# First batch by pairs of heads on a queue of its own, dummy products early, 4-byte products spread wider

## The chip, the cores and the metric

The kernel runs on one core of a Trainium2 chip. The time is device microseconds of one execution, from the launch's first to its last instruction with what lies around them; lower is better. Before the change the median of three runs is 395.43 us (393.86 to 397.88).

## The reference: linear attention, then a gated mixer of tokens and channels

Eight batches, eight heads, 576 tokens, head width 64, so a model width of 512 and a hidden width of 2048. All inputs and the output are float32.

```python
# attention, for each batch and head
kv  = k.T @ v                                  # 64 x 64, no softmax
o   = q @ kv                                   # 576 x 64
x   = o / sqrt(mean(o * o, axis=-1) + 1e-6) * g_norm
# heads side by side: x is 576 x 512 for each batch
tok = w_tok @ (alpha1 * x + beta1)             # over the 576 tokens
u   = x + lam * tok
ch  = relu((alpha2 * u + beta2) @ w_ch1) @ w_ch2   # 512 -> 2048 -> 512
out = u + lam * ch
```

## The kernel before

**Layout.** Of a batch's 576 tokens, 512 stand as four rows on each of 128 partitions (token 4p + c is row c of partition p). The last 64 are the tail; tails of two batches share a tile. q, k and v are used as 4-byte fp32r operands of TensorE, everything after the norm as bf16.

**A recorded program.** Every operation is put on record with what it reads and writes, its cost in a table and its priority. `schedule` (line 109) then plays the five engines against that table and writes out one fixed order for each; `synchronize` adds the semaphore waits, and `emit` the instructions. On the chip each engine goes through its order and waits where it must: an instruction that waits holds up all behind it on its engine. A number in the table changes only the order.

**Two streams on TensorE.** "main" is the channel mixer: `ch1` (line 900, 64 products of 512 columns for a batch), `ch1_tail` (line 913, in odd batches) and `ch2` (line 928, 64, and 16 more for the tails). "fill" is the rest, taken up where its inputs are there: `kv` (lines 616 and 621, 20 products a batch), `qtr` (lines 668 and 650, q transposed through a product with the identity, 20), `norm` (lines 701 and 727, q times kv, 20), `tok` (line 800, 20 of 512 columns) and `tok_tail` (line 818). The attention and token mixing of batch b+2 are filled into the channel mixer of batch b. An operation of many 4-byte products (`slow=True`) is woven with one of the main stream, product by product (`woven`, line 293): four with four alternate, the ten of half a `kv` come two or three at a time.

**After a product.** ScalarE squares (line 755), VectorE sums, inverts, scales into `xm` (line 766) and multiplies with e1 into bf16 `rm` or `rtl` (line 770). GpSimd multiplies `xm` with g_norm (line 778). `bias1` (line 786) and the result of `tok` (line 807) are added on VectorE. From batch 2 on, GpSimd makes a2 in two steps (lines 878 and 881) and a transposing DMA puts it where `ch1` reads it; in batches 0 and 1 TensorE transposes (line 838). After `ch2` VectorE scales (line 944), GpSimd adds (line 949), SP stores.

**The head of the program** is batch 0, with no main stream to fill. SP's queue loads q whole, then k and v in two halves of four heads each, as float32; VectorE and ScalarE round k and v to fp32r (lines 599 and 602). GpSimd's queue loads, and converts, the weights: two quarters of w_ch1 at once, and w_tok when the second half of k has landed. Six rows are broadcast over the partitions by products with a row of ones (line 555): e1, g, e2, lam, a2 and b2. `columns` (line 564) turns two rows into columns. Five `wt_group`s transpose w_tok (lines 974 and 976); its row sums are products with a column of ones (lines 1004 and 1008) and wait for all of w_tok. Then come `tok` of batch 0 in two halves of 256 columns (line 800), the transposes of line 838, and the main stream. Batch 1's k and v come as float32 through SP, into the same buffers as batch 0's, and are rounded by VectorE and ScalarE too; later batches come through GpSimd's queue, already as fp32r.

Of the kernel before, what the change touches and what calls it, by code (L numbers as in the profile page):

```python
# [16 lines left out]
DH = 64  # L17
# [35 lines left out]
class Prog:  # L53
    ENGINES = ("PE", "ACT", "DVE", "POOL")

    def __init__(self, nc, stack):
        self.nc, self.stack = nc, stack
        self.ops, self.lastw, self.readers = [], {}, {}
        self.ps = stack.enter_context(nc.psum_tensor("ps", [128, 8, 512], F32))
        self.eng = {"PE": nc.tensor, "ACT": nc.scalar, "DVE": nc.vector,  # L60
                    "POOL": nc.gpsimd, "SP": nc.sync}
        self.pools = {"main": (0, 1, 2, 3), "fill": (4, 5, 6, 7), "any": tuple(range(8))}
        self.main, self.fill = [], []
        self.bias = 0.0
        self.dma_rate = 360e3

# [3 lines left out]
    def _add(self, o, r, w, after):  # L70
        self.ops.append(o)
        for key in r:
# [48 lines left out]
    def schedule(self):  # L121
# [15 lines left out]
        last_fill = False  # L137
# [52 lines left out]
        while left:  # L190
            moved = True
            while moved:
                moved = False
                for e, q in queues.items():
                    if free[e] > t + 1e-9:
                        continue
                    for o in q[:160]:
# [8 lines left out]
                if free["PE"] <= t + 1e-9:  # L206
                    m = main[0] if main and can(main[0], t) else None
                    f = None
                    if not (last_fill and m):
                        for o in fill[:10]:  # L210
# [6 lines left out]
                    if f is not None and m is not None and f.kind == "w":  # L217
# [5 lines left out]
                        take(m, t, cost)  # L223
                        free["PE"] = t + cost
                        self.sequence.append((f, m))
                    elif f is not None:
                        fill.remove(f)
                        take(f, t)
                        free["PE"] = t + f.cost
                        self.sequence.append((f,))  # L230
                        last_fill = True
                    elif m is not None:
# [3 lines left out]
                        self.sequence.append((m,))  # L236
                    else:
                        continue
                    events.add(free["PE"])
# [12 lines left out]
    def synchronize(self):  # L252
# [25 lines left out]
        for unit in self.sequence:  # L278
            for o in unit:
                wait_for(o)  # L280
            for o in self.ended(unit):
# [11 lines left out]
    def woven(f, m):  # L293

        out, i, j = [], 0, 0
        n, k = len(f.fns), len(m.fns)
        while i < n or j < k:
# [3 lines left out]
            else:  # L301
                out.append((m, j))
# [3 lines left out]
    def ended(self, unit):  # L306
        if len(unit) == 1:
            return unit
        f, m = unit
        return (m, f) if self.woven(f, m)[-1][0] is f else (f, m)  # L310

    def emit(self):
# [8 lines left out]
        for unit in self.sequence:  # L321
            for o in self.ended(unit):
# [21 lines left out]
        def _(gps):  # L344
            for unit in self.sequence:
                if len(unit) == 1:
                    o, = unit
                    waits(o)
                    for fn in o.fns:
                        ins = fn(self.eng[o.q])  # L350
                    signal(o, ins)
                    continue
                begun = set()
                for o, i in self.woven(*unit):
                    if o.idx not in begun:
                        begun.add(o.idx)
                        waits(o)
                    ins = o.fns[i](nc.tensor)
# [7 lines left out]
def bass_transnormer_attn__then__resmlp_affine_kernel(  # L366
# [15 lines left out]
    with ExitStack() as stack:  # L382
# [7 lines left out]
        identb = sb("identb", [128, 128], BF16)  # L390
        ones = sb("ones", [128, 128], F32)
# [75 lines left out]


        P.bias = -1000.0
        P.op("DVE", dve(2), lambda e: e.memset(eps[:], 64e-6), w=["eps"])  # L470
# [10 lines left out]
        for i in range(2):  # L481
            P.op("POOL", pool(1024, 0), lambda e, i=i: e.memset(kvc[:, i].bitcast(F32), 0.0),
                 w=[("kvc", i, j) for j in range(2)])
# [7 lines left out]
        P.dma("SP", "q", 1 << 20, lambda e: e.dma_start(md(q0), src_main(q, 0, 0, 8)),  # L491
              w=["q0"])
        P.dma("SP", "qtl", 1 << 17, lambda e: e.dma_start(q0t, src_tail(q, 0, 0, 8)),
              w=["q0t"])
        first = {}
        for h in range(2):
            a, z = 4 * h, 4 * h + 4
            for n, x, m, tl in (("k", k, kst, kstt), ("v", v, vst, vstt)):
                first[n, h] = P.dma("SP", "%sm%d" % (n, h), 1 << 19,
                                    lambda e, x=x, m=m, a=a, z=z: e.dma_start(  # L500
                                        md(m[:, a:z]), src_main(x, 0, a, z)),
                                    w=[("st", n, h)])
                P.dma("SP", "%st%d" % (n, h), 1 << 16, lambda e, x=x, tl=tl, a=a, z=z:
                      e.dma_start(tl[:, a:z], src_tail(x, 0, a, z)), w=[("stt", n, h)])
        for i, x in enumerate((moe_alpha1, moe_lam, moe_beta1, moe_alpha2, moe_beta2)):
            P.dma("ACT", "row%d" % i, 2048, lambda e, i=i, x=x: e.dma_start(
                rows[0:1, i, :], x[None, :]), w=[("row", i)])
        P.dma("ACT", "row5", 256, lambda e: e.dma_start(rows[0:1, 5, 0:DH], g_norm[None, :]),
              w=[("row", 5)])
# [4 lines left out]
            w=["wl"], after=[first["k", 1]], issue=1.2)  # L514
# [15 lines left out]

        load_w1(0)
        load_w1(1)
# [20 lines left out]
        def broadcast(i, dst, key, n=DM):  # L553
            t = P.bank("fill")
# [6 lines left out]
        def columns():  # L561

            t = P.bank("fill")
# [8 lines left out]
        def fill_q(b):  # L572

            if b > 1:
                load_kv(b)
# [6 lines left out]
        def load_kv(b):  # L582
            for n, x, m, tl in (("k", k, kr, krt), ("v", v, vr, vrt)):
                P.dma("POOL", n + "r", 1 << 20, lambda e, x=x, m=m: e.dma_start(
                    md(m[:]), src_main(x, b, 0, 8)), w=[(n, 0), (n, 1)], issue=1.2)
# [3 lines left out]
        def round_kv(h, both=False):  # L589
            a, z = (0, 8) if both else (4 * h, 4 * h + 4)  # L590
            hs = (0, 1) if both else (h,)
# [546 lines left out]
```

## Time and profile before

| what | value |
|---|---|
| median of three runs | 395.43 us |
| the profiled execution | 393.75 us, of which the span is 391.9 us |
| TensorE busy | 365.0 us, 93% of the span |
| VectorE, ScalarE, GpSimd busy | 195.2, 163.0, 198.6 us |
| first product of the channel mixer | 57.92 us after the span's start |
| last product | ends at 387.28 us |
| read from HBM, written | 38.04 MB, 9.44 MB |

A busy TensorE is not one at its peak: a product counts from its start to its modelled end, so neighbours overlap, and a product at half clock is as busy as one at full clock. The spacing from one start to the next says more. The granted clock is printed as full from the start; where the spacing says otherwise, the text goes by the spacing.

### The profile page before, as it was taken

How to read it: one execution, taken by the hardware profiler on the slowest of the kernel's cores; microseconds unless marked ns; L12 is line 12 of the kernel's file. 1: busy time of each engine (PE TensorE's matmuls, PEld its weight loads, DVE VectorE, ACT ScalarE, POOL GpSimd, SP SyncE). 2: the span in 40 equal slices, each digit the busy share in tenths (PEclk: the TensorE clock that was granted, in tenths of full speed). 3: DMA queues.
4: the chain of work that ended last, by engine and by line, in shares of the span. 5: the costliest groups of instructions: out<-in, count | busy, mean ns of one | idle time of the engine just before them, and what ended most of it. 6: DMA issues, size and time to landing. Idle time of an engine off the chain costs nothing.

```text
span 391.9 us, 5426 instructions
## 1 busy us (share of the span) xinstructions
PE 365.0 (93%) x2163; PEld 219.4 (56%) x2163; DVE 195.2 (50%) x329; ACT 163.0 (42%) x323; POOL 198.6 (51%) x180
## 2 busy tenths in 40 slices
PE   3568799999999998998999998899999999999995
PEld 3344678545768566466565774756444644444642
DVE  3244871894259479758849647255970020010042
ACT  3243617901695145472186252446017305406500
POOL 7112604332526996898897697564878131031000
PEclk9999999999999999999999999899999999999999
DMA  8999587900492965659649149801103021020012
GB/s 229 229 232 316 84 134 142 221 2 9 139 302 36 269 138 131 125 107 253 147 83 240 26 102 259 178 16 40 55 29 79 15 80 56 0 79 30 2 54 80
DMA packets 62118, 46.52 MB, mean 119 GB/s; under 512 B 28615, under 2 KB 57351, under 8 KB 62092
## 3 DMA queue, kind: packets, MB, share of 16 engines
q0 software_dynamic: 34240, 27.27, 40.3%
q1 hardware_dynamic: 27840, 18.88, 18.8%
q8 instruction: 17, 0.28, 0.3%
q14 instruction: 9, 0.07, 0.1%
q10 hardware_dynamic: 12, 0.01, 0.0%
HBM read 38.04 MB, written 9.44 MB: 121 GB/s over the span
## 4 chain that ended last, share of the span: by engine, by line
PE 72%; DVE 11%; DMA 8%; POOL 3%; issue 2%; ACT 2%; SPq 2%
PE ps L928 25%; PE ps L900 24%; PE ps L800 8%; DMA xm<-in_v_dram 4%; DMA vrt<-in_v_dram 4%; PE ps L913 3%; PE ps L616 3%; DVE rm L770 3%; PE ps L701 2%; PE ps L668 2%; POOL a1f L878 2%; PE ps L555 1%; DVE xm L766 1%; DVE small L758 1%; DVE rtl L770 1%
## 5 line engine op out<-in xcount | busy, mean ns | idle before, releaser
L900 PE MATMUL ps<-a2m,w 128*128 128x512 bf16 x512 | 132.3, 386 | 0.0
L928 PE MATMUL ps<-w,ht 128*128 128x512 bf16 x512 | 127.5, 382 | 0.0
L895 ACT ACTIVATE ht<-ps 128x512 bf16<-128x512 f32 x128 | 76.2, 598 | 84.3 <-PE ps L900 83.0
L928 PEld LDWEIGHTS ps<-w,ht 128*128 128x128 bf16 x512 | 49.3, 98 | 51.7 <-issue 0.4
L900 PEld LDWEIGHTS ps<-a2m,w 128*128 128x128 bf16 x512 | 49.2, 98 | 48.8 <-issue 0.8
L944 DVE TENSOR_TENSOR tmp<-ps,lam_bc 128x512 f32<-128x512 f32 x36 | 24.8, 688 | 97.9 <-PE ps L928 97.8
L949 POOL TENSOR_TENSOR xm<-xm,tmp 128x512 f32<-128x512 f32 x28 | 37.1, 1326 | 57.5 <-DVE tmp L944 57.4
L778 POOL TENSOR_TENSOR xm<-xm,g_bc 128x512 f32<-128x512 f32 x32 | 43.6, 1374 | 31.9 <-DVE rm L770 31.8
L758 DVE TENSOR_REDUCE small<-sq 128x8 f32<-128x512 f32 (+2 forms) x41 | 26.8, 661 | 39.8 <-ACT sq L755 39.7
L878 POOL TENSOR_TENSOR a1f<-xm,a_bc 128x512 f32<-128x512 f32 x24 | 30.1, 1271 | 17.2 <-DVE xm L807 17.2
L701 PE MATMUL ps<-kvc,qt 128*128 128x128 f32 x128 | 37.6, 412 | 1.2 <-ACT lam_bc L558 1.2
L616 PE MATMUL ps<-vr,kr 128*128 128x128 f32 x128 | 27.5, 349 | 10.5 <-ACT vrt L602 3.8
L800 PE MATMUL ps<-rm,wt 128*128 128x512 bf16 (+1 forms) x144 | 35.2, 372 | 0.7 <-DVE rtl L770 0.5
L881 POOL TENSOR_TENSOR a2b<-a1f,b_bc 128x512 bf16<-128x512 f32 x27 | 34.1, 1271 | 0.3
L786 DVE SCALAR_TENSOR_TENSOR xm<-e_bc,wsum,xm 128x512 f32<-128x512 f32 (+1 forms) x36 | 32.4, 942 | 1.6 <-POOL xm L778 1.4
L668 PE MATMUL ps<-identr,qr 128*128 128x128 f32 x112 | 32.0, 395 | 1.3 <-DVE kvc L632 1.3
L616 PEld LDWEIGHTS ps<-vr,kr 128*128 128x128 f32 x128 | 24.2, 220 | 13.6 <-DMA vrt<-in_v_dram 4.4
L755 ACT ACTIVATE sq<-ps 128x512 f32<-128x512 f32 (+2 forms) x41 | 23.5, 582 | 14.5 <-PE ps L701 9.4
L673 ACT ACTIVATE qt<-ps 128x512 fp32r<-128x512 f32 x32 | 19.2, 600 | 24.6 <-PE ps L668 19.0
L701 PEld LDWEIGHTS ps<-kvc,qt 128*128 128x128 f32 x128 | 26.2, 217 | 4.5 <-ACT kvc L635 1.5
L770 DVE TENSOR_TENSOR rm<-xm,e_bc 128x512 bf16<-128x512 f32 x32 | 27.2, 862 | 0.1
L807 DVE TENSOR_TENSOR xm<-ps,xm 128x512 f32<-128x512 f32 (+1 forms) x36 | 21.5, 624 | 10.8 <-PE ps L800 10.6
(107 smaller groups left out, 396.3 us busy)
## 6 DMA issues: line engine op xcount, KB each, us to landing
out_dram<-xm SPq DMA_DIRECT2D x32, 256.0 KB, 2.4
qr<-in_q_dram POOLq DMA_DIRECT2D x7, 1024.0 KB, 11.0
kr<-in_k_dram POOLq DMA_DIRECT2D x6, 1024.0 KB, 6.8
vr<-in_v_dram POOLq DMA_DIRECT2D x6, 1024.0 KB, 9.5
w<-in_moe_w_ch_dram POOLq DMA_DIRECT2D x8, 512.0 KB, 10.2
ht<-in_q_dram SPq DMA_DIRECT2D x1, 1024.0 KB, 5.6
xm<-in_k_dram SPq DMA_DIRECT2D x2, 512.0 KB, 9.9
xm<-in_v_dram SPq DMA_DIRECT2D x2, 512.0 KB, 12.7
```

The lines of the kernel that those rows point to most:

```text
L616: fns += [lambda e, h=h, o=o, c=c: e.matmul(t.ap()[:, o], fl(kr[:, h, c:c + 2, :]), fl(vr[:, h, c:c + 2, :]), start=(h % 4 == 0 and c == 0 ...
L668: fns.append(lambda e, h=h, c=c, o=o: e.matmul(t.ap()[:, o], fl(qr[:, h, c:c + 2, :]), identr[:], start=True, stop=True))
L701: fns = [lambda e, h=h: e.matmul(t.ap()[:, 128 * (h % 4):128 * (h % 4) + 128], qt[:, h, cp, :], kvc[:, i, h, :], start=True, stop=True) fo ...
L770: P.op("DVE", dve(n), lambda e: e.tensor_tensor(out=r, in0=x, in1=bc(e1_bc[rs, fs]), op=ALU.mult), r=xks + ["e1"], w=rks)
L778: P.op("POOL", pool(n), lambda e: e.tensor_tensor(out=hv(gx), in0=hv(gx), in1=gv, op=ALU.mult), r=xks + ["g"], w=xks)
L800: lambda e, sc=sc: e.matmul(t.ap()[:, cs], wt[:, sc if sc < 4 else tail_w(b), 128 * c:128 * c + 128], (rm[:, b % 2, sc, cs] if sc < 4 else ...
L878: P.op("POOL", pool(512), lambda e: e.tensor_tensor(out=a1f[:, s], in0=x, in1=a2_bc[:], op=ALU.mult), r=ks + ["a2"], w=[("a1f", s)])
L881: P.op("POOL", pool(512), lambda e: e.tensor_tensor(out=a2b[:, c], in0=a1f[:, s], in1=b2_bc[:], op=ALU.add), r=[("a1f", s), "b2"], w=[("a2 ...
L895: P.op("ACT", act(512), lambda e: e.activation(dst, t.ap(), ACT.Relu), r=[t], w=keys, pri=-1000)
L900: P.mm("main", 512, [lambda e, dj=dj: e.matmul(t.ap(), w1[:, dj, 128 * fj:128 * fj + 128], a2m[:, b % 3, dj, :], start=(dj == 0), stop=(dj ...
L928: P.mm("main", 512, [lambda e, fj=fj, t=t, c=c: e.matmul(t.ap(), (ht[:, fj, 128 * c:128 * c + 128] if c < 4 else hl[:, fj, :]), w2[:, fj, ...
L949: lambda e: e.tensor_tensor(out=x, in0=x, in1=tmp[:, s], op=ALU.add),
```

## The change

**First batch by pairs of heads.** k, v and q of batch 0 come as four DMAs each, of two heads, in the order k, v, q for each pair, behind the two tails, all on SP's queue. w_tok now waits for the third pair of k, and the w_ch1 quarters are recorded later, behind it. `round_kv`, `kv`, `qtr` and `norm` work on a pair of heads in batch 0. `kv` is recorded as a group of four products for each pair and a group of one or two for the tails, in all batches. `norm` takes one pair with all four rows, where it took four heads with two rows.

**Fewer steps in the head.** lam, a2 and b2 are loaded by broadcasting DMAs once the third quarter of w_ch1 has landed. The row sums of w_tok are taken group by group, each with its own wait. Batch 1's k and v come through GpSimd's queue as in later batches, without rounding. In batch 0 GpSimd makes two of the four `rm`. The second half of the tail's transposed w_tok is written by ScalarE.

**Dummy products.** A zeroed 128x256 bf16 tile is multiplied with itself on TensorE, with nobody reading the result, wherever the schedule sees TensorE idle before the first true product: 47 products.

**The weave.** A group of more than two 4-byte products for batch b+2 is spread over two operations of the main stream, eight products, where a second one is ready. The cost table is changed: a woven 4-byte product counts 74 ns, or 58 ns where spread over two, and early products count double. DMAs of GpSimd's queue keep the order in which they are recorded. Work of batch 0 may use seven PSUM banks instead of four.

```diff
-                        cost = sum(max(len(o.fns) * 0.056, o.cost * (0.53 if o is f else 1))
-                                   for o in (f, m))
+                        cost = m.cost + 0.074 * n
...
+                        if (n > 2 and f.pri // 100 - (m.pri - 150) // 100 > 1 and m2 is not None and not m2.narrow
+                                and can(m2, t + cost)):
+                            main.pop(0)
+                            unit.append(m2)
+                            take(m2, t + cost, m2.cost - 0.016 * n)
+                            cost += m2.cost - 0.016 * n
...
+                    elif self.warm is not None and t >= self.warm[0].end and not begun:
+                        o = Op("PE", "m", 0.11, 0.0, [self.warm[1]], 0.0, len(self.ops))
...
+        P.warm = (P.op("DVE", dve(256), lambda e: e.memset(warm[:], 0.0), w=["warm"]),
+                  lambda e: e.matmul(P.ps[:, 3, 0:256], warm[:, 0:128], warm[:],
+                                     start=True, stop=True))
...
+        def pair_dma(eng, n, x, m, hp):
+            first[n, hp] = P.dma(eng, "%s%d" % (n, hp), 1 << 18, lambda e: e.dma_start(
+                md(m[:, 2 * hp:2 * hp + 2]), src_main(x, 0, 2 * hp, 2 * hp + 2)),
+                w=[("st", n, hp)])
...
+        for hp in range(4):
+            pair_dma("SP", "k", k, kst, hp)
+            pair_dma("SP", "v", v, vst, hp)
+            pair_dma("SP", "q", q, q0, hp)
...
-            w=["wl"], after=[first["k", 1]], issue=1.2)
+            w=["wl"], after=[first["k", 2]], issue=1.2)
...
-        load_w1(0)
-        load_w1(1)
...
+            for hp in hps:
+                fns = []
+                for h in (2 * hp, 2 * hp + 1):
...
+                P.mm("fill", 128, fns, r=[("k", hp), ("v", hp)], w=[t], slow=True)
...
+            swap = b == 0 and hp in (0, 2)
+            P.op("POOL" if swap else "DVE", pool(n) if swap else dve(n),
+                 lambda e: e.tensor_tensor(out=r, in0=x, in1=bc(e1_bc[rs, fs]), op=ALU.mult),
+                 r=xks + ["e1"], w=rks, pri=-300 if swap else 0)
...
-        P.op("DVE", dve(8), lambda e: e.memset(wsum[:], 0.0),
-             r=[("wtm", i) for i in range(6)] + ["wt45"], w=["wt", "wsum0"])
...
-        broadcast(1, lam_bc, "lam")
-        broadcast(3, a2_bc, "a2")
-        broadcast(4, b2_bc, "b2")
...
+        load_w1(0)
+        load_w1(1)
+        fill_q(1)
         load_w1(2)
         load_w1(3)
-        fill_q(1)
         for i in range(4):
             load_w2(i)
+        for x, dst, key in ((moe_lam, lam_bc, "lam"), (moe_alpha2, a2_bc, "a2"),
+                            (moe_beta2, b2_bc, "b2")):
+            P.dma("SP", "b" + key, 1 << 18, lambda e, x=x, dst=dst: e.dma_start(
+                dst[:], x.partition_broadcast(128)), w=[key], after=[wdma[2]])
...
+        P.cold = 22.0
```

In the rows of an order below, `ht` and `xm` hold the float32 q, k and v of batch 0, `kr`, `vr` and `qr` the fp32r ones, `w` any of the weights or rows; `128x2x256` is two heads on 128 partitions.

SP's queue at the start of the program, before:

```order
L491 DMA ht<-in_q_dram 128x8x256
L493 DMA ht<-in_q_dram 64x8x64
L500 DMA xm<-in_k_dram 128x4x256
L504 DMA xt<-in_k_dram 64x4x64
L500 DMA xm<-in_v_dram 128x4x256
L504 DMA tmp<-in_v_dram 64x4x64
L500 DMA xm<-in_k_dram 128x4x256
```

and after:

```order
L541 DMA xt<-in_k_dram 64x8x64
L545 DMA tmp<-in_v_dram 64x8x64
L537 DMA xm<-in_k_dram 128x2x256
L537 DMA xm<-in_v_dram 128x2x256
L537 DMA ht<-in_q_dram 128x2x256
L537 DMA xm<-in_k_dram 128x2x256
L537 DMA xm<-in_v_dram 128x2x256
```

Whole q no longer stands ahead of k and v; the last pair of q is the last of the fifteen loads. On GpSimd's queue the first DMA is now w_tok's, behind its wait for the third pair of k; the w_ch1 quarters, which stood ahead of it without a wait, follow it.

TensorE from its first true product on; before (identity and `ht` are q's transposes, `vr,kr` is `kv`, `w,ones` a broadcast, `kvc,qt` is `norm`):

```order
L665 MATMUL ps<-ident,ht 128x128 x16
L645 MATMUL ps<-ident,ht 128x64 x4
L616 MATMUL ps<-vr,kr 128x128 x8
L621 MATMUL ps<-vrt,krt 128x2x64 x2
L555 MATMUL ps<-w,ones 128x512
L555 MATMUL ps<-w,ones 128x64
L555 MATMUL ps<-w,ones 128x512
L701 MATMUL ps<-kvc,qt 128x128 x8
L727 MATMUL ps<-kvc,qtt 128x128 x2
L616 MATMUL ps<-vr,kr 128x128 x8
L621 MATMUL ps<-vrt,krt 128x2x64 x2
L555 MATMUL ps<-w,ones 128x512 x3
```

and after, around the last pair of q (`ht` in the third row) and the first of five groups of w_tok's transpose (`identb`):

```order
L657 MATMUL ps<-vr,kr 128x128 x4
L665 MATMUL ps<-vrt,krt 128x2x64
L711 MATMUL ps<-ident,ht 128x128 x4
L657 MATMUL ps<-vr,kr 128x128 x4
L747 MATMUL ps<-kvc,qt 128x128 x4
L665 MATMUL ps<-vrt,krt 128x2x64
L1023 MATMUL ps<-identb,ht 128x128 x4
L1025 MATMUL ps<-identb,hl 128x64
```

and behind the fifth group (`ones,w` is `columns`, `onesb,wt` the row sums):

```order
L747 MATMUL ps<-kvc,qt 128x128 x4
L772 MATMUL ps<-kvc,qtt 128x128 x2
L596 MATMUL ps<-w,ones 128x512
L605 MATMUL ps<-ones,w 128x1 x8
L1054 MATMUL ps<-onesb,wt 128x1 x4
L1057 MATMUL ps<-onesb,wt 64x1 x2
```

Behind the last pair of q stand now one `kv`, two `norm`s, w_tok's transposes, one broadcast of 512 columns, `columns` and the row sums; then `tok` of batch 0.

TensorE in the channel mixer, `kv` of a later batch, before:

```order
L616 MATMUL ps<-vr,kr 128x128 x2
L900 MATMUL ps<-a2m,w 128x512
L616 MATMUL ps<-vr,kr 128x128 x3
L900 MATMUL ps<-a2m,w 128x512
L616 MATMUL ps<-vr,kr 128x128 x2
```

and after, batch 3's `kv` in batch 1's `ch2` (line 977 now):

```order
L665 MATMUL ps<-vrt,krt 128x2x64
L977 MATMUL ps<-w,ht 128x512 x2
L665 MATMUL ps<-vrt,krt 128x2x64
L977 MATMUL ps<-w,ht 128x512 x2
L657 MATMUL ps<-vr,kr 128x128
L977 MATMUL ps<-w,ht 128x512 x2
```

and the end of batch 3's attention, ahead of batch 2's `ch1` (line 949 now):

```order
L714 MATMUL ps<-identr,qr 128x128
L977 MATMUL ps<-w,hl 128x512
L714 MATMUL ps<-identr,qr 128x128 x4
L696 MATMUL ps<-identr,qrt 128x64 x4
L747 MATMUL ps<-kvc,qt 128x128 x16
L949 MATMUL ps<-a2m,w 128x512 x4
```

A 4-byte product has two of the main stream between it and the next, where it had one or stood in a cluster. At the end of batch 3's attention 24 stand alone: batch 1's `ch2` has no product left there, and batch 2's `ch1` stands behind them. Over the whole program the fill of the last batch ends some 210 main products later than before.

More of the change, by code (lines that the diff above doesn't have):

```diff
@@ L196, in schedule @@
                         continue
-                    for o in q[:160]:
+                    held = False
+                    for o in list(q):
+                        if o.kind == "d":
+                            if held:
+                                continue
+                            held = e == "POOL"
                         if can(o, t):
@@ L278, in synchronize @@
         for unit in self.sequence:
-            for o in unit:
-                wait_for(o)
-            for o in self.ended(unit):
+            for o, first, last in self.steps(unit):
+                if first:
+                    wait_for(o)
+                if not last:
+                    continue
                 count[o.q] += 1
@@ L292, in woven @@
     @staticmethod
-    def woven(f, m):
+    def woven(unit):
+        if len(unit) == 1:
+            return [(unit[0], i) for i in range(len(unit[0].fns))]
+        f = unit[0]
+        rest = [(o, i) for o in unit[1:] for i in range(len(o.fns))]
         out, i, j = [], 0, 0
-        n, k = len(f.fns), len(m.fns)
+        n, k = len(f.fns), len(rest)
         while i < n or j < k:
@@ L301, in woven, with steps @@
             else:
-                out.append((m, j))
+                out.append(rest[j])
                 j += 1
         return out
[L306 to L310, printed above, removed]
+    def steps(self, unit):
+        return [(o, i == 0, i == len(o.fns) - 1) for o, i in self.woven(unit)]
     def emit(self):
@@ L321, in emit @@
         for unit in self.sequence:
-            for o in self.ended(unit):
+            for o, _, last_one in self.steps(unit):
+                if not last_one:
+                    continue
                 if o.kind == "d":
@@ L639, in qtr @@
         def qtr(b, hp):
[L641 removed]
+            t = P.bank(where[0])
             if hp == 4:
@@ L996, in bass_transnormer_attn__then__resmlp_affine_kernel @@
[L996 removed]
+        round_kv(4)
+        for hp in range(4):
+            qtr(0, hp)
+            round_kv(hp)
+            kv(0, (hp,))
+            if hp == 1:
+                qtr(0, 4)
+            norm(0, hp)
+            if hp % 2:
+                norm(0, 5 + hp // 2)
         for sc in range(5):
             wt_group(sc)
[L999 to L1001 removed]
@@ L1002, in bass_transnormer_attn__then__resmlp_affine_kernel @@
-        fns = []
-        for c in range(4):
-            fns += [lambda e, c=c, sc=sc: e.matmul(
+        broadcast(7, e2_bc, "e2")
+        columns()
+        t = P.bank(where[0])
+        for sc in range(5):
+            fns = [lambda e, c=c, sc=sc: e.matmul(
                 t.ap()[:, c:c + 1], wt[:, sc, 128 * c:128 * c + 128], onesb[:, 0:1],
-                start=(sc == 0), stop=(sc == 4)) for sc in range(5)]
-        for i in range(2):
+                start=(sc == 0 and c == 0), stop=False) for c in range(4)]
```

330 lines of the change are left out of this document (160 added, 170 removed).

## The prediction

> **What bounds the kernel now.** First the page: the engines' busy time, and what one step of a kind takes.
>
> ```profile
> PE 365.0 (93%) x2163; PEld 219.4 (56%) x2163; DVE 195.2 (50%) x329; ACT 163.0 (42%) x323; POOL 198.6 (51%) x180
> ...
> L949 POOL TENSOR_TENSOR xm<-xm,tmp 128x512 f32<-128x512 f32 x28 | 37.1, 1326 | 57.5 <-DVE tmp L944 57.4
> ...
> L878 POOL TENSOR_TENSOR a1f<-xm,a_bc 128x512 f32<-128x512 f32 x24 | 30.1, 1271 | 17.2 <-DVE xm L807 17.2
> ```
>
> No engine but TensorE is near its limit over the whole. Next the waits of TensorE from 57 us to the end (total, times, longest), and the end of the chain of waits in order of time (start, length):
>
> ```profile
> PE ps L616 <- DMA vrt<-in_v_dram: 3.4, 2, 2.3
> PE ps L668 <- DVE kvc L632: 1.3, 1, 1.3
> PE ps L800 <- DVE rtl L770: 0.5, 1, 0.5
> ```
>
> ```profile
> 352.61 13.81 PE ps L900 x64
> ```
>
> In 330 us TensorE waits 5.2 us; it goes through its order, a 512-column product each 13.81 / 64 = 0.2158 us. From about 50 us on, only fewer or cheaper products shorten the kernel. What else can go is the stretch ahead. So third, the head, from the timeline (start, length, in brackets the idle time before):
>
> ```profile
> 6.36 3.68 PE L665 MATMUL ps<-ident,ht 128*128 128x128 f32 x16 [6.36 <-DMA ht<-in_q_dram]
> 9.07 0.69 DVE L599 CAST kr<-xm 128x1024 fp32r<-128x1024 f32 x1 [5.42 <-DMA xm<-in_k_dram]
> 14.47 1.97 PE L616 MATMUL ps<-vr,kr 128*128 128x128 f32 x8 [3.82 <-ACT vrt L602]
> 24.11 1.06 ACT L602 ACTIVATE vr<-xm 128x1024 fp32r<-128x1024 f32 x1 [1.53 <-DMA xm<-in_v_dram]
> 26.30 0.41 ACT L602 ACTIVATE vrt<-tmp 64x256 fp32r<-64x256 f32 x1
> 27.43 1.97 PE L616 MATMUL ps<-vr,kr 128*128 128x128 f32 x8 [3.15 <-ACT e_bc L558]
> 29.20 0.63 PE L621 MATMUL ps<-vrt,krt 128*128 128x128 f32 x2
> 29.75 5.48 PE L555 MATMUL ps<-w,ones 1*128 1x512 f32 x6
> 38.93 3.57 PE L564 MATMUL ps<-ones,w 1*128 1x1 f32 x16
> 42.44 0.62 PE L974 MATMUL ps<-identb,ht 128*128 128x128 bf16 x4
> 45.89 0.26 PE L976 MATMUL ps<-identb,hl 64*64 64x64 bf16 x1
> 48.12 0.69 PE L1004 MATMUL ps<-onesb,wt 128*128 128x1 bf16 x20 [1.97 <-DVE wsum L999]
> 55.61 1.04 PE L838 MATMUL ps<-ident,xm 128*128 128x128 f32 x8
> ```
>
> The second half of v lands at 24.11 and its tail at 26.30. Behind it stand `kv`, six broadcasts, `norm`, `columns`, w_tok's transposes, a round trip to VectorE and the row sums: `tok` of batch 0 ends only at 55.6. And fourth, `tok` alone in two windows (us, TensorE busy, count, loads, granted clock, DMA share, GB/s):
>
> ```profile
> 49.17:53.41 4.24, 4.24 (x20) 3.02 (x21) 1.00 1.17 164
> 53.41:55.60 2.19, 2.19 (x21) 1.87 (x19) 1.00 1.22 205
> ```
>
> The same products at 0.212 us, then at 0.109: the clock doubled at 53.4, though the granted clock is printed as full throughout. Likewise sixteen fp32 transposes take 3.68 us at 6.36, eight 1.04 at 55.61. The head runs at half clock, and the nearly unbroken work from 27.43 to 46.15 did not end that.
>
> **The change: the loads.** Fifth view, DMA in windows (last column GB/s):
>
> ```profile
> 2.00:8.60 6.60, 2.24 (x11) 2.24 (x12) 1.58 (x4) 1.59 (x4) 6.12 (x10) 1.00 1.05 289
> 8.60:24.00 15.40, 11.25 (x37) 7.35 (x35) 4.18 (x9) 5.03 (x10) 2.13 (x3) 1.00 1.18 233
> 44.60:56.40 11.80, 9.83 (x89) 7.80 (x88) 10.25 (x21) 4.30 (x6) 4.88 (x5) 1.00 1.14 176
> 61.90:63.70 1.80, 1.80 (x16) 1.52 (x15) 0.42 (x1) 1.71 (x4) 1.71 (x3) 1.00 0.03 6
> 63.80:76.20 12.40, 12.40 (x78) 7.95 (x77) 6.25 (x13) 11.74 (x25) 4.92 (x6) 1.00 1.71 283
> ```
>
> and a load's issue on GpSimd:
>
> ```profile
> 61.99 0.88 POOL L584 DMA_DIRECT2D kr<-in_k_dram  x1 [12.50 <-PE ps L621]
> ```
>
> SP alone moves 289 GB/s. Once the w_ch1 quarters run beside it, k and v from 9.07 to 24.11 (1.77 MB) come at 118. q, k and v of a batch are 3.54 MB. Alone they would move from 2.0 to 14.2; 1.05 MB of q, by that rate there at 5.6, were seen at 6.36, so 0.7 us for the landing. The third pair of k (2.23 MB in) lands at 10.4; w_tok is asked for then, and packets come 1.8 us later, as the window at 61.90 shows for a load that GpSimd issued at 61.99. By 12.2, 2.95 MB are through. The other 0.59 MB at 118 GB/s take 5.0: the last pair of q at 17.9. Bounds: 15 alone; 21 if w_tok's 4 us hold SP's queue as they held the v tail (64 KB from 24.11 to 26.30, 30 GB/s). I take 19, since w_tok goes first.
>
> **Dummies.** 47 at 0.212 are 10.0 us, from 1.3 to 11.3; if the clock doubles after 4.24 us of them, as it did from 49.17 to 53.41, twenty take 4.24 and the rest 27 x 0.109, and they end at 8.5. The work of the first three pairs stands behind them, about 11 us at half clock by the durations of the next paragraph (three transposes 2.8, three `kv` with tails 3.9, two `norm` and a tail 2.6, two broadcasts and q's tail under 2). So TensorE is ready for the last pair between 14 (all of that at full clock) and 22 (nothing at full clock). Their cover is that pair's landing at 19; where it is gone they cost up to 3. I take nothing.
>
> **The chain behind the last pair**, at half clock: four transposes 0.92 (3.68 / 4), `kv` 0.99 and its tail 0.32, `norm` 0.99, w_tok's transposes 3.71 (42.44 to 46.15), `norm` 0.99 and its tail 0.63, one broadcast 0.91, `columns` 3.57, row sums 1.05 (48.12 to 49.17): 14.1, so `tok` starts at 33.1 and ends 6.43 later, at 39.5. Before: 55.6. **Gain 16.1.** The five broadcasts fewer (4.6), the rounding and the round trip are in this. On VectorE, the copy of `columns` (32.0) stands ahead of the last pair's scaling:
>
> ```profile
> 38.35 0.69 DVE L766 TENSOR_TENSOR xm<-ps,small 128x512 f32<-128x512 f32 x1
> 43.67 2.39 DVE L770 TENSOR_TENSOR rtl<-xt,e_bc 64x256 bf16<-64x256 f32 x1
> ```
>
> With two reciprocals, `xm`, `xt`, `rm` and `rtl` some 4.7 us: 36.7. The first half of `tok` covers it until 37.3. GpSimd's two `rm` and its issues: batch 1's k and v are asked for after the last `kv`, behind w_tok and the two quarters (1.7 MB, done at about 24 by 115 beside SP and 176 alone); 2.36 MB at 283 land at 33, against a use at 39.5. The quarters of w_ch1 and w_ch2 that follow end near 56, as before; their first use there is past 59.
>
> **The weave.** Sixth view, TensorE's timeline:
>
> ```profile
> 100.30 0.39 PE L900 MATMUL ps<-a2m,w 128*128 128x512 bf16 x1
> 103.98 0.39 PE L900 MATMUL ps<-a2m,w 128*128 128x512 bf16 x1
> 104.27 0.39 PE L900 MATMUL ps<-a2m,w 128*128 128x512 bf16 x1
> 108.35 0.39 PE L900 MATMUL ps<-a2m,w 128*128 128x512 bf16 x1
> ...
> 113.77 0.39 PE L900 MATMUL ps<-a2m,w 128*128 128x512 bf16 x1
> 114.06 2.12 PE L900 MATMUL ps<-a2m,w 128*128 128x512 bf16 x9
> 115.83 0.41 PE L727 MATMUL ps<-kvc,qtt 128*128 128x128 f32 x1
> 116.08 0.39 PE L900 MATMUL ps<-a2m,w 128*128 128x512 bf16 x1
> ```
>
> 100.30 to 103.98 is a clustered `kv`: 8 main products and 20 of 4 bytes, (3.68 - 1.73) / 20 = 0.098 each. From 104.27 they alternate, 14 and 14: (4.08 - 3.02) / 14 = 0.076. From 113.77, two stand nine main products apart: (2.31 - 2.16) / 2 = 0.076. So breaking up clusters saves 0.022, 20 times in six batches, **2.6**; a second main product between them saves nothing more. (Were the cost table's 16 ns real, some 216 spread products would give 3.5 more; a loss has no row.) The 24 that stand alone before batch 2's `ch1` lose 0.022 each, **0.5**.
>
> **New waits.** The transposing DMA, from the DMA view (us each):
>
> ```profile
> a2m<-a2b SPq DMA_TRANSPOSE x24, 2.5
> ```
>
> Batch 2's `ch1` needs GpSimd's eight steps of 1.27 and three additions of 1.33 after the first `tok`, about 1 of VectorE and 2.5 for the transposing DMA: 17.7. TensorE has 67 products of 512 columns, 20 woven and 24 alone for that time: 14.5 + 1.5 + 2.4 = 18.4. A wait of 0 to 3; I take 1. Batch 4's k and v are asked for only behind these steps, at about 15.4; with 1.8 and 8.3 us they land at 25.5, TensorE wants them 4 main operations in, near 22.5: 3. With 1 elsewhere that is the 5.2 of before, so nothing net.
>
> **Sum:** 393.75 (span 391.9 and 1.85 around it) - 16.1 - 2.6 + 0.5 = 375.5. The median of before is 1.7 above its profiled execution, within its scatter of 4; the forecast is **376**.
>
> **Rivals.**
>
> *The dummies lift the clock and it holds.* Then the chain halves to about 7.1, VectorE's 4.7 after `columns` ends near 30, and half of `tok` behind it at 32.5, close to the landing of batch 1's v at 33. Gain 23, time 369. For: `tok` lifted the clock by itself in 4.24 us, and dummies are such products. Against: the pairs leave TensorE gaps, and
>
> ```profile
> 248.00:251.40 3.40, 3.40 (x16) 3.08 (x14) 0.42 (x1) 0.98 (x2) 2.03 (x2) 0.50 1.00 198
> ```
>
> after a wait of less than 3 us shows 0.50 granted. [...] Chance 0.15.
>
> *The queue gives less.* w_tok and the small DMAs hold the last pair to 24 us: 381. For: 30 GB/s in that stretch. Against: 289 alone. Chance 0.14.
>
> *The main stream waits for its inputs, and it is slower.* The fill ends some 210 main products later, and between `tok` and `ch1` lie 17.7 us of GpSimd and DMA. If that lands 5 us late in each of batches 2 to 7, 30 us: 406. It is slower than before from 3.7 us a batch on: without the 4 us of such waits in it the sum is 371.5, and (393.75 - 371.5) / 6 = 3.7. For: in batch 2 the margin is 0.7. Against: in the other batches the order leaves 40 main products or more, and GpSimd is busy 51%. Chance 0.05 for more than 4.6 us a batch, and 0.05 for the 3.3 to 4.6 that end within 1% of before.
>
> **Numbers.** Forecast 0.61, the rivals 0.15, 0.14, 0.05 and 0.05. The range reaches from below the second case to above the third, with 3.5 for the weave and 3 for waits: 367 to 386. About 1% (4 us) is what a measurement of this kernel can tell. Faster by over that 0.90, same 0.05, slower 0.05.
>
> **What would show it.** The last pair of q transposed at 17 to 21 us; `tok` of batch 0 from about 33, its first products at 0.21 spacing; batch 2's `kv` spread at 0.076; waits after 45 us of 4 to 7. A `tok` at 0.109 from its start means the first rival; a start after 37 the second; TensorE waits over 20 us the third.

## The result and the profile after

The changed kernel takes **377.34 us** (median of four, 376.05 to 378.12) against 395.0 for the kernel before: a ratio of 0.9539, with a 95% interval from 0.9481 to 0.9597. Run once more beside the experiments, the ratio was 0.9539 again (0.9507 to 0.9570). The forecast was 376, the range 367 to 386. The profiled execution took 377.47, its span 375.7.

First TensorE's waits from 45 us to the end (total, times, longest):

```profile
PE ps L949 <- DMA a2m<-a2b: 4.4, 1, 4.4
PE ps L849 <- DVE xm L856: 1.1, 1, 1.1
```

With 0.2 elsewhere TensorE waits 5.7 us where it waited 5.2, most of it in one piece ahead of batch 2's `ch1`. The head in the timeline (lines 501 dummies, 711 q's transposes, 747 `norm`, 657 `kv`, 1023 w_tok's transposes, 596 a broadcast, 605 `columns`, 1054 row sums, 849 `tok`):

```profile
1.05 7.15 PE L501 MATMUL ps<-warm 128*128 128x256 bf16 x47 [1.05 <-DVE eps L503]
8.52 0.66 PE L711 MATMUL ps<-ident,ht 128*128 128x128 f32 x4 [0.32 <-DMA ht<-in_q_dram]
14.53 1.11 PE L747 MATMUL ps<-kvc,qt 128*128 128x128 f32 x4 [1.31 <-ACT kvc L681]
19.34 1.07 PE L711 MATMUL ps<-ident,ht 128*128 128x128 f32 x4
...
22.03 0.65 PE L1023 MATMUL ps<-identb,ht 128*128 128x128 bf16 x4
...
27.17 2.07 PE L596 MATMUL ps<-w,ones 1*128 1x512 f32 x2
29.04 3.41 PE L605 MATMUL ps<-ones,w 1*128 1x1 f32 x16
32.38 0.27 PE L1054 MATMUL ps<-onesb,wt 128*128 128x1 bf16 x4
34.11 1.04 PE L849 MATMUL ps<-rm,wt 128*128 128x256 bf16 x4
...
40.78 1.09 PE L657 MATMUL ps<-vr,kr 128*128 128x128 f32 x8
```

The last pair of q is transposed at 19.34, `tok` of batch 0 starts at 34.11 (before: 49.17) and gives way to the next work at 40.78 (before: 55.61): 14.8 us of the gain lie in the head. From there to the last product the kernel before took 387.27 - 55.61 = 331.7, this one 370.98 - 40.78 = 330.2: 1.5 for the weave with all that follows from it. Windows of the head (TensorE busy and count, granted clock, DMA share, GB/s):

```profile
1.05:4.87 3.82, 3.81 (x18) 1.00 0.56 142
4.87:8.28 3.41, 3.33 (x30) 1.00 0.99 305
8.28:11.70 3.42, 2.94 (x16) 1.00 1.12 267
11.70:39.00 27.30, 25.99 (x148) 0.50 1.35 233
```

The first window prints 1.00, but 18 dummies in 3.82 us are 0.212 each: half clock, as the records begin only at the first rise. Among the dummies the clock doubled at 4.87 (3.33 / 30 = 0.111 each after it); it fell at 11.70, with TensorE busy 2.94 of the last 3.42 us, and came back at 39.00, within `tok`.

### The profile page after: what moved, and what is told of

The parts are those of the page before. It is cut to its first block, busy times and chain, and to the rows that moved or that the text cites. A ratio compares the mean times of both kernels' runs of the same rounds, so it can differ in the third digit from the quotient of the medians.

```text
span 375.7 us, 5460 instructions
## 1 busy us (share of the span) xinstructions
PE 360.6 (96%) x2169; PEld 218.4 (58%) x2204; DVE 183.6 (49%) x327; ACT 162.6 (43%) x324; POOL 205.9 (55%) x186
## 4 chain that ended last, share of the span: by engine, by line
PE 87%; DMA 4%; DVE 4%; SPq 2%; issue 1%; POOL 1%; ACT 0%
PE ps L977 33%; PE ps L949 28%; PE ps L849 9%; PE ps L962 4%; PE ps L747 3%; PE ps L657 2%; DMA a2m<-a2b 2%; DMA xm<-in_v_dram 2%; PE ps L714 2%; PE ps L867 1%; SPq L537 1%; PE ps L887 1%; PE ps L605 1%; PE ps L772 1%; DVE xm L833 1%
## 5 line engine op out<-in xcount | busy, mean ns | idle before, releaser
L949 PE MATMUL ps<-a2m,w 128*128 128x512 bf16 x497 | 129.6, 388 | 5.1 <-DMA a2m<-a2b 4.4
L977 PE MATMUL ps<-w,ht 128*128 128x512 bf16 x497 | 124.2, 382 | 0.8
L949 PEld LDWEIGHTS ps<-a2m,w 128*128 128x128 bf16 x512 | 44.2, 99 | 50.1 <-DMA a2m<-a2b 4.2
L977 PEld LDWEIGHTS ps<-w,ht 128*128 128x128 bf16 x512 | 37.7, 98 | 35.2 <-issue 0.4
L657 PE MATMUL ps<-vr,kr 128*128 128x128 f32 x128 | 44.0, 390 | 0.0
L747 PE MATMUL ps<-kvc,qt 128*128 128x128 f32 x128 | 39.3, 390 | 1.3 <-ACT kvc L681 1.3
L714 PE MATMUL ps<-identr,qr 128*128 128x128 f32 x112 | 39.4, 394 | 0.0
L833 DVE SCALAR_TENSOR_TENSOR xm<-e_bc,wsum,xm 128x512 f32<-128x512 f32 (+1 forms) x36 | 27.7, 824 | 3.6 <-POOL xm L825 3.5
L747 PEld LDWEIGHTS ps<-kvc,qt 128*128 128x128 f32 x128 | 24.4, 212 | 7.2 <-ACT kvc L681 1.5
L800 ACT ACTIVATE sq<-ps 128x512 f32<-128x512 f32 (+2 forms) x41 | 23.4, 583 | 10.8 <-PE ps L747 10.1
L714 PEld LDWEIGHTS ps<-identr,qr 128*128 128x128 f32 x112 | 20.8, 193 | 9.0
```

The lines of the kernel that those rows point to most:

```text
L657: fns += [lambda e, h=h, o=o, c=c: e.matmul(t.ap()[:, o], fl(kr[:, h, c:c + 2, :]), fl(vr[:, h, c:c + 2, :]), start=(h == h0 and c == 0), ...
L714: fns.append(lambda e, h=h, c=c, o=o: e.matmul(t.ap()[:, o], fl(qr[:, h, c:c + 2, :]), identr[:], start=True, stop=True))
L747: fns = [lambda e, h=h, cp=cp: e.matmul(t.ap()[:, 256 * (h % 2) + 128 * cp:256 * (h % 2) + 128 * cp + 128], qt[:, h, cp, :], kvc[:, i, h, ...
L833: P.op("DVE", dve(128 * len(hps) + 50), lambda e: e.scalar_tensor_tensor(out=x, in0=e2_bc[:, fs], scalar=wsum[:, c:c + 1], in1=x, op0=ALU. ...
L949: P.mm("main", 512, [lambda e, dj=dj: e.matmul(t.ap(), w1[:, dj, 128 * fj:128 * fj + 128], a2m[:, b % 3, dj, :], start=(dj == 0), stop=(dj ...
L977: P.mm("main", 512, [lambda e, fj=fj, t=t, c=c: e.matmul(t.ap(), (ht[:, fj, 128 * c:128 * c + 128] if c < 4 else hl[:, fj, :]), w2[:, fj, ...
```

## The experiments

Gains and losses are given against the changed kernel, by the difference of the two ratios to the kernel before times 395.4.

### What the dummies are worth

```diff
+        P.sequence = [u for u in P.sequence if u[0].fns[0] is not P.warm[1]]
```

> The changed kernel with its 47 dummy products taken out of the finished order, everything else in its place. As the prediction has it (dummies cost nothing and the landing of the last pair sets the chain behind it): 377.3, no change. Second theory: that chain started at 19.34 because TensorE was late, not the load, and the dummies' full clock from 4.87 to 11.70 shortened the work of the first pairs. At half clock the 2.9 us of products between 8.52 and 11.7 take 2.9 longer, less the two waits of 0.24 and 1.31 behind them: the last q pair is transposed about 1.3 later, 20.7, and the time is 378.7. The spacing is 0.21 from the first product on in both.

Measured: 377.72, ratio 0.9589 (0.9558 to 0.9619). That is 2 us over the changed kernel by ratio and 0.4 to 0.9 by the medians, so the time alone does not decide between the two theories. In its timeline:

```profile
8.23 1.11 PE L711 MATMUL ps<-ident,ht 128*128 128x128 f32 x4 [8.23 <-DMA ht<-in_q_dram]
...
11.71 1.11 PE L657 MATMUL ps<-vr,kr 128*128 128x128 f32 x4
```

The first pairs take longer, since all is at half clock, but the last pair of q is transposed at 19.43, against 19.34. What the full clock gained until 11.70 the changed kernel gave back in the wait of 1.31 for ScalarE's `kvc`, which stood behind the rounding of the third pair of v:

```profile
13.52 0.63 ACT L641 ACTIVATE vr<-xm 128x512 fp32r<-128x512 f32 x1 [1.71 <-DMA xm<-in_v_dram]
14.17 0.31 ACT L681 ACTIVATE kvc<-kvc 64x128 fp32r<-64x128 f32 x1
```

Without dummies TensorE arrives later and does not wait. The trace has `tok` end 0.4 later, because the clock rose at 39.76 instead of 39.00. So the second theory's 1.3 in the chain did not appear, and by the trace the dummies bring next to nothing, as the prediction took them; the times leave room for up to some 2 us.

### Which work lifts the clock

```diff
-        warm = sb("warm", [128, 256], BF16)
+        warm = sb("warm", [128, 128], F32R)
...
-                  lambda e: e.matmul(P.ps[:, 3, 0:256], warm[:, 0:128], warm[:],
+                  lambda e: e.matmul(P.ps[:, 3, 0:128], warm[:], warm[:],
```

> The 47 dummies are 4-byte products of 128x128 instead of 2-byte products of 128x256; both have spacings of 0.21 at half clock and 0.11 at full. If any unbroken work of TensorE lifts the clock, it doubles within 3.5 to 7 us of the first dummy as before and the time stays at 377.3. If the clock goes by the rows that the array streams in a window of 3.41 us (a 4-byte product streams 128 where a 2-byte one streams 256 in the same time), the spacing stays at 0.21, the dummies end at 11.1 instead of 8.2, the first pair starts 2.5 late and at half clock: the last q pair is transposed at 23 and the time is 381.

Measured: 380.33, ratio 0.9653 (0.9618 to 0.9689), 4.5 slower.

```profile
1.05 10.29 PE L501 MATMUL ps<-warm 128*128 128x128 f32 x47 [1.05 <-DVE eps L503]
22.29 1.07 PE L711 MATMUL ps<-ident,ht 128*128 128x128 f32 x4
```

Forty-seven unbroken 4-byte products in 10.1 us, 0.215 each to the end: TensorE was busy without a gap for all of that time, and the clock stayed at half until 40.67. The last pair comes at 22.29, where 23 was expected. Work without a gap was not enough here; with the 2-byte dummies, as unbroken, the clock had doubled after 3.82 us. The last section sets the two beside other stretches.

### Holding the clock through the head

```diff
...
+            for _ in range(2 if n < 18 else 8 if len(o.fns) in (1, 8) else 3):
+                d = Op("PE", "m", 0.11, 0.0, [P.warm[1]], 0.0, len(P.ops))
+                d.end = o.end
+                P.ops.append(d)
+                seq.append((d,))
...
```

> About 95 more 2-byte dummies stand between the steps of the first batch, two to eight behind each, up to its token mixing. If rows streamed per window hold the clock (windows that lost it in the traces so far streamed 39% of the full rate or less, windows that kept it 47% or more), TensorE stays at full clock from 4.87 on: the last q pair is transposed near 17, the token mixing starts near 26 instead of 34.1 and takes 4.4 instead of 6.7, and batch 1's loads become the next bound at about 31: time 367 to 370, the prediction's first rival. If the clock falls again at 11.7 for another reason, the dummies stand at 0.21 each between the steps: at least 12 us more, 389 or above.

Measured: 380.29, ratio 0.9654 (0.9620 to 0.9687), 4.5 slower: neither the 367 to 370 nor the 389 of the two theories. Its windows (busy time and count of TensorE, its weight loads, VectorE, ScalarE, GpSimd; then clock, DMA share, GB/s) and three rows of its timeline:

```profile
14.00:30.50 16.50, 16.20 (x138) 12.75 (x137) 8.40 (x20) 13.04 (x31) 12.04 (x13) 1.00 1.38 239
30.50:40.70 10.20, 10.20 (x72) 8.13 (x72) 3.73 (x11) 0.00 (x0) 6.30 (x8) 0.50 1.37 184
```

```profile
18.53 0.60 PE L711 MATMUL ps<-ident,ht 128*128 128x128 f32 x4
32.28 1.89 PE L501 MATMUL ps<-warm 128*128 128x256 bf16 x8
38.89 1.06 PE L849 MATMUL ps<-rm,wt 128*128 128x256 bf16 x4
```

The clock theory held over most of the head: the clock was full from 6.62 to 30.52. The time that went with it did not come. The dummies filled what the clock gave (the last pair at 18.53, only 0.8 earlier), and from 27.6 on TensorE had a broadcast and `columns`, products of one row, and at 30.52 the clock fell; the 23 dummies that stood behind them then cost 0.21 each. So the dummies held the clock for 23.9 us here, and took the time that it gave. What a clock that holds without them would be worth, the 7 us of the first rival, no run shows.

### The order of the loads

```diff
+        first_w1 = [u for u in P.sequence if u[0].slot in ("w1_0", "w1_1")]
+        P.sequence = [u for u in P.sequence if u not in first_w1]
+        at = next(i for i, u in enumerate(P.sequence) if u[0].slot == "wl")
+        P.sequence[at:at] = first_w1
```

> The first two quarters of w_ch1 go ahead of w_tok on GpSimd's queue again, without a wait, as in the kernel before; nothing else moves. If the order of the loads is what the head gained by, SP falls from some 300 GB/s to 118 from about 7 us on (2.3 MB to go), the last pair of q lands near 26 instead of 16, w_tok behind it, and the chain behind starts 6.5 later than 19.34: token mixing at 40.5, time 383 to 384. If TensorE's backlog at half clock hides most of it, or the queues share better with transfers this small, the start moves less than 3 and the time stays below 380.

Measured: 382.05, ratio 0.9670 (0.9635 to 0.9705), 5.2 slower.

```profile
19.13 1.12 PE L747 MATMUL ps<-kvc,qt 128*128 128x128 f32 x4 [6.94 <-ACT kvc L681]
23.94 1.07 PE L711 MATMUL ps<-ident,ht 128*128 128x128 f32 x4
38.71 1.04 PE L849 MATMUL ps<-rm,wt 128*128 128x256 bf16 x4
```

With the w_ch1 quarters on the way, TensorE waits 6.9 us from 12.2 on (ScalarE's `kvc` stands behind the rounding of the third pair of v, which now begins at 18.12 instead of 13.52), and the chain starts 4.6 later, where 6.5 was expected. The last pair of q, issued at 11.2 and 9.7 on the way, was there at 20.9 and not at 26. Of the 15.1 us by which `tok` starts earlier than in the kernel before, the hold on w_ch1 is 4.6.

### What a broadcast costs

```diff
+        broadcast(1, lam_bc, "lam")
+        broadcast(3, a2_bc, "a2")
+        broadcast(4, b2_bc, "b2")
...
-        for x, dst, key in ((moe_lam, lam_bc, "lam"), (moe_alpha2, a2_bc, "a2"),
-                            (moe_beta2, b2_bc, "b2")):
-            P.dma("SP", "b" + key, 1 << 18, lambda e, x=x, dst=dst: e.dma_start(
-                dst[:], x.partition_broadcast(128)), w=[key], after=[wdma[2]])
```

> lam, a2 and b2 are broadcast by products with a row of ones again, instead of three DMAs: two of them stand behind columns, ahead of w_tok's row sums, one among the dummies; the rest is planned as in the changed kernel. The prediction counted 0.91 for a broadcast at half clock; the changed kernel's row of one broadcast shows two instructions and 1.87 from start to start. If TensorE's order sets the start of the token mixing and a broadcast is two instructions, it starts 3.7 later, near 37.9, and the time is 380.5. By 0.91 each: 1.8 later, 378.7. If ScalarE's and VectorE's work on w_tok and rm sets the start, no change: 377.

Measured: 380.30, ratio 0.9619 (0.9589 to 0.9648), 3.2 slower.

```profile
32.40 3.76 PE L596 MATMUL ps<-w,ones 1*128 1x512 f32 x4
37.82 1.04 PE L849 MATMUL ps<-rm,wt 128*128 128x256 bf16 x4
```

One of the three stands among the dummies again, the other two behind `columns`. These two are four instructions and take 3.68 from their start to the row sums; `tok` starts 3.71 later. A float32 broadcast of 512 columns is two instructions of 0.92, not one, and TensorE's order sets the start of `tok`. If this 3.7 and the 4.6 of the loads add, 6.8 of the 15.1 remain that no run takes out one by one: the work by pairs, the rounding, the round trip to VectorE, the two `rm` on GpSimd.

### columns ahead of the first pair

```diff
...
-            for i in (0, 1, 5, 2, 3, 4):
+            for i in (3, 4, 0, 1, 5, 2):
...
         broadcast(5, g_bc, "g", DH)
+        broadcast(7, e2_bc, "e2")
+        columns()
...
-        broadcast(7, e2_bc, "e2")
-        columns()
...
+        P.sequence = [u for u in P.sequence if u[0].fns[0] is not P.warm[1]]
```

(The planner's figures for the landing of the small rows and for the length of `columns` were set so that it places it there.)

> No dummies; columns stands ahead of the first pair of q, in the time that TensorE otherwise waits or does dummies (its two rows are loaded first), and e2's broadcast beside e1's. The rest is planned as in the changed kernel. If TensorE's own work at half clock sets the start of the token mixing (it worked without a break from 14.5 to 34.1 while all of q, k and v was there at 16), columns' 3.4 and about 1 of the broadcast leave that stretch: the token mixing starts near 29.5 to 30.5 instead of 34.1, and the time is 3.5 to 4.5 less, 373. If ScalarE and VectorE set it (in the changed kernel the last rm was ready at 34.3, and ScalarE wrote the last of w_tok at 28.4), the start moves less than 1.5 and the time stays above 375.5.

Measured: **373.54** (372.70 to 374.36), ratio 0.9454 (0.9425 to 0.9483): 3.4 faster than the changed kernel.

```profile
2.55 3.57 PE L608 MATMUL ps<-ones,w 1*128 1x1 f32 x16 [2.55 <-DMA w<-in_moe_beta_dram]
8.80 4.21 PE L599 MATMUL ps<-w,ones 1*128 1x64 f32 x6
20.65 1.07 PE L714 MATMUL ps<-ident,ht 128*128 128x128 f32 x4
30.39 1.03 PE L852 MATMUL ps<-rm,wt 128*128 128x256 bf16 x4
```

`columns` now runs where the dummies ran, and `tok` starts at 30.39. The last pair comes 1.3 later, as the broadcasts stand ahead of the first `kv`. The theory that ScalarE and VectorE set the start of `tok` allowed it 1.5 earlier; it came 3.7 earlier. So from the last pair on TensorE's own work is the bound of the head, and real work in its early idle time is worth what dummies there were not.

### The weave

The changed kernel, without an edit, ran beside these two and the one with columns early.

> The changed kernel once more, beside the three that are compared with it on the same chip: 0.954 of the kernel before (0.948 to 0.960 measured so far), about 376 to 378.

Measured: 376.87, ratio 0.9539. No spread over a second main operation, in the same order:

```diff
+        P.sequence = [v for u in P.sequence for v in ([u[:2], u[2:]] if len(u) > 2 else [u])]
```

> In the finished order every four 4-byte products that were spread over eight of the main stream alternate with the first four of them, and the other four follow alone (216 products); nothing else moves. As the prediction has it, a 4-byte product costs 0.076 between two main ones and as much with a second main product behind it (in the changed kernel's trace: main, 4-byte, main 281 against 216, and 10 more for the next main one; alternating 291 against 216): no change, within 0.5 of the changed kernel. By the cost table's 16 ns a product: 3.5 slower.

Measured: 377.66, ratio 0.9554 (0.9523 to 0.9586): 0.6 slower, within the noise; 3.5 is excluded. In the traces the way from the end of `tok` to the last product is 330.1 us against 330.2 for the changed kernel. And the 4-byte products in clusters:

```diff
-            if i < n and (j >= k or i * k <= j * n):
+            if i < n:
```

> All woven 4-byte products (390, in groups of one, two and four) stand together ahead of the main products they were woven with; nothing else moves. If a cluster costs what the clusters of two and three cost in the kernel before (0.094 and 0.099 a product against 0.075), the time is 386 x 0.025 = 9 to 10 longer than the changed kernel's. If those clusters were dear for another reason (their weights, or what kv waits for), the time stays within 2.

Measured: 386.15, ratio 0.9770 (0.9736 to 0.9805): 9.1 slower, 9.1 / 386 = 0.024 a product. A group of `kv` in the changed kernel, and the same in this one:

```profile
109.00 0.61 PE L977 MATMUL ps<-w,ht 128*128 128x512 bf16 x2
109.25 0.41 PE L657 MATMUL ps<-vr,kr 128*128 128x128 f32 x1
109.50 0.60 PE L977 MATMUL ps<-w,ht 128*128 128x512 bf16 x2
109.76 0.41 PE L657 MATMUL ps<-vr,kr 128*128 128x128 f32 x1
110.01 0.61 PE L977 MATMUL ps<-w,ht 128*128 128x512 bf16 x2
```

```profile
109.06 0.75 PE L657 MATMUL ps<-vr,kr 128*128 128x128 f32 x4
109.65 1.90 PE L977 MATMUL ps<-w,ht 128*128 128x512 bf16 x8
111.20 0.74 PE L657 MATMUL ps<-vr,kr 128*128 128x128 f32 x4
```

From 109.00 to 110.01 stand four main products and two of 4 bytes: (1.01 - 4 x 0.2158) / 2 = 0.073 each. From 109.06 to 111.20 stand eight and four: (2.14 - 8 x 0.2158) / 4 = 0.103. The price lies in 4-byte products that follow each other; whether one or two main ones separate them made no difference.

### The wait ahead of batch 2's ch1

In the changed kernel's chain of waits (start, length):

```profile
127.56 1.24 POOL a2b L930
...
128.82 7.48 DMA a2m<-a2b
```

The last transposing DMA takes 7.48; its median is 2.5. Batch 4's first load is issued at 128.74, in its company. The clock falls within the wait and is half for 6.83 us, 134.58 to 141.40. The edit makes that load wait for the DMA:

```diff
+        kr4 = next(o for o in P.ops if o.slot == "kr" and o.pri == 300)
+        last = next(o for o in P.ops if o.slot == "t3" and o.pri == 250)
+        kr4.deps.add(last)
+        kr4.raw.add(last)
+        P.sequence.remove((kr4,))
+        P.sequence.insert(P.sequence.index((last,)) + 1, (kr4,))
```

> Batch 4's first load of k waits on GpSimd until the last transposing DMA of batch 2 has landed; all else as in the changed kernel. There TensorE waited 4.4 us for that DMA, issued at 128.82 and landed at 136.3, and ran 6.8 us at half clock behind the wait. Theory one: the loads issued from 128.74 on stretched the transposing DMA from 2.5 to 7.5. Then it lands near 131.5, the wait and the half clock go, and 4.4 + 3.4 = 7.8 come back, less up to 3 where batch 4's k and v come later: 370 to 373. Theory two: the chain through GpSimd is late of itself, and the DMA needs its 7.5 in any company: 377.3 or, with the loads later, up to 379.

Measured: 380.02, ratio 0.9656 (0.9613 to 0.9699): 4.6 slower, where the first theory had 370 to 373. GpSimd's load, and TensorE's waits from 45 us on:

```profile
130.41 0.94 POOL L624 DMA_DIRECT2D kr<-in_k_dram  x1 [2.72 <-DMA a2m<-a2b]
```

```profile
PE ps L657 <- DVE xt L811: 5.1, 1, 5.1
PE ps L772 <- DVE xm L811: 1.8, 1, 1.8
```

The DMA, issued at 127.71, now lands at 130.4, 2.7 later: the loads were what stretched it, and the wait for it is gone. But 6.9 us of waits for VectorE stand in its place. Batch 3's `norm` is a run there (sixteen products at 129.2), so its tiles come to VectorE all at once, and `kv` of the next batch waits for the last of them. That VectorE used the wait of 4.4 in the changed kernel to catch up fits this, and is argued, not shown. Half clock follows here too, from 139.3 on (two `ch1` products take 1.08 at 142.44 and 0.60 at 146.26). In this trace, of the fastest of the four executions, the way from the end of `tok` to the last product is 332.7 against 330.2; the rest of the 4.6 stays open. With no weave over a second main operation in the planner that run does not arise:

```diff
-                        m2 = main[0] if main else None
+                        m2 = None
```

> The changed kernel with the weave over a second main operation switched off in the planner (its costs and all else as changed); the order is planned anew: batch 2's token mixing begins 16 main products earlier, batch 3's norm alternates with the main stream instead of standing in a run of 16 to 20, and the last token mixing ends some 160 main products earlier. If the looser weave is what makes batch 2's a2 late, the wait of 4.1 to 4.4 before its ch1 shrinks by 16 products' time (about 4) and the 6.8 us at half clock behind it (3.4 lost) go: 370. If the wait only changes its place, as it did when batch 4's loads were held back (380.0), 376 to 378. If the second main operation was worth the cost table's 16 ns a product, 380.

Measured: 378.92, ratio 0.9582 (0.9551 to 0.9614): 1.7 slower, at the edge of the noise, and not the 7 faster of the first theory.

```profile
PE ps L949 <- DMA a2m<-a2b: 3.0, 1, 3.0
PE ps L849 <- DVE rtl L817: 1.9, 3, 0.7
PE ps L657 <- DMA vr<-in_v_dram: 1.4, 2, 1.3
```

The wait before `ch1` shrinks to 3.0 and half clock to 3.41, but 3.3 of other waits come up; with 0.8 for VectorE's `xm` they are 7.1 in all. Why the planner's new order waits more elsewhere was not followed up. Both together, on the kernel with columns early:

```diff
-                        m2 = main[0] if main else None
+                        m2 = None
```

> columns early and no dummies (373.5 alone), and no weave over a second main operation, together. Where the two act in different places, they add: with 370 for the second alone, 366.5. If the second one alone is worth nothing, 373.5.

Measured: 375.30 (372.48 to 377.93), ratio 0.9498 (0.9454 to 0.9542). They do not add: by ratio this is 1.7 slower than columns early alone, with intervals that overlap. The profiled execution, at 372.48, is the fastest of the six.

```profile
PE ps L660 <- DMA vr<-in_v_dram: 5.4, 3, 3.0
PE ps L852 <- DVE rtl L820: 1.2, 2, 0.6
PE ps L852 <- DVE xm L859: 0.7, 1, 0.7
```

In this order the clock stays full from 34.18 to the end and a2 is never late, yet TensorE waits 7.3 us, now for v. In each of the three orders 7 to 8 us of waits came up, under other names. What would remove them stays open; the fastest version measured here is columns early alone.

## Why the prediction was right, step by step

**Loads: the right start from the wrong cause.** The last q pair was put at 19 by its landing. It was transposed at 19.34, with no wait in front of it:

```profile
9.78 0.85 SPq L537 DMA_DIRECT2D ht<-in_q_dram  x1
```

```profile
ht<-in_q_dram SPq DMA_DIRECT2D x4, 256.0 KB, 6.4
```

Issued at 9.78 and some 6.4 on the way, it was there at about 16, near the lower bound of 15 that I gave for SP alone. The third pair of k landed later than the 10.4 of the forecast, so w_tok was asked for only at 13.05, and it met only the last of SP's loads; the 5.0 us of a shared queue did not come. What set 19.34 was the other side, "TensorE is ready between 14 and 22": it worked without a break from 14.53. That this side ended at 19.34, beside the 19 of the landing, is luck. Without the hold on w_ch1 that side gives way to the loads again (23.94).

**Dummies, taken as nothing:** confirmed by the trace, and by the times to within 2 us. The cover was not the landing but the wait for `kvc`.

**The chain, 14.1:** measured 34.11 - 19.34 = 14.8. Two terms were mis-sized. The broadcast was counted as 0.91, from the row of six instructions in 5.48, which are three broadcasts; one took 27.17 to 29.04, 1.87. The row sums, 1.05 when they stood together, took 32.38 to 34.11, 1.73, group by group. The other terms came out 0.95 shorter than counted. The same misreading is in "five broadcasts fewer (4.6)": three stood behind the second half of v before, one stands in the chain now, and two are worth 3.7, as the two that came back showed. This number was not a term of the sum. `tok`, counted as 6.4, took 6.7 to 40.78, as the clock doubled 4.9 after its start and not 4.24; what sets that moment no run shows. In two other traces with the same work there `tok` took 5.7 (batch 4's loads held back: the clock rose 2.9 after its start) and 7.2 (clusters: 5.9 after), so traces with the same work there lie up to 1.5 us apart. Head: 14.8 for 16.1.

**The weave, 2.6 less 0.5:** mechanism right (0.024 for each product out of a cluster, nothing for the second main product), and 1.5 measured for all that follows the head, with 0.5 more of waits and 3.4 more at half clock in it (134.58 to 141.40, for 247.98 to 251.39 before). The diff also lets the planner look through 60 operations of the fill instead of 10. The pieces were not separated further.

**Waits, no change:** 5.7 for 5.2, but by other terms than I listed. Batch 2's `ch1` waited 4.4 where I took 1, past the bound of 3, because the transposing DMA was priced at its median of 2.5; batch 4's loads, taken as 3, did not show; the 1 elsewhere came out at 1.3. The sum came out right by errors that offset each other, which is luck; three later orders moved these waits about and did not remove them.

**Rivals.** The dummies did lift the clock, and it did not hold (full from 4.87 to 11.70). The queue gave no less than forecast: the last pair was there at 16, not at 17.9. The main stream did not wait: 5.7 us in all, not 20. Of the 2.0 between the sum (375.5) and the profiled 377.47, 1.3 is the head and 0.6 the rest.

## What to carry to other kernels

Look for idle time early on the engine that bounds the head and put real work there: dummies were worth 0 to 2 us, `columns` in the same place 3.4. Count instructions, not operations, when a row is priced (a float32 broadcast of 512 columns was two, 0.92 each). And where one engine waits a few us in a long run, ask which other engine may catch up in that time before the wait is removed: three times other waits came up in its place.

## What the chip showed that was not expected

The clock did not follow how busy TensorE was. From the traces' clock records (start, length, clock):

```
kernel before    53.42 194.56 1.0 | 247.98 3.41 0.5 | 251.39 139.95 1.0
changed kernel   4.87 6.83 1.0 | 11.70 27.31 0.5 | 39.00 95.57 1.0 | 134.58 6.83 0.5 | 141.40 232.11 1.0
4-byte dummies   (half until 40.67) | 40.67 95.57 1.0 | 136.25 6.83 0.5 | 143.07 232.11 1.0
clock held       6.62 23.89 1.0 | 30.52 10.24 0.5 | 40.76 95.57 1.0 | 136.33 6.83 0.5 | 143.16 235.52 1.0
```

Two stretches of the kernel before (TensorE busy and count, clock, DMA share, GB/s):

```profile
148.99:152.40 3.41, 2.10 (x15) 1.00 0.53 109
244.56:247.98 3.42, 1.74 (x13) 1.00 1.57 346
```

The first had a wait of 1.3 us in it and kept the clock, the second lost it at 247.98. The stretch from 8.28 to 11.70 in the changed kernel's head was busier than both, 2.94 us, and lost the clock too. Per us, the columns of the products that start in these three stretches are 3840 / 3.41 = 1126, 3200 / 3.42 = 936 and 2688 / 3.42 = 786. At half clock, the 2-byte dummies had 18 x 256 columns in 3.82 us, 1206, when the clock rose; the 4-byte ones had 47 x 128 in 10.05 us without a gap, 599, and it did not rise. So in these five stretches the columns fall in line with what the clock did, and the busy time does not. No run varies the columns alone: what sets the clock is not shown.

A transposing DMA, 2.5 us in the median, took 7.5 when loads of GpSimd's queue were issued with it, and 2.7 when they were held back.
